# Talking-heads attention with a mixture of experts: w1 of the first expert is loaded two steps apart, and the last tokens' ranks, logits and row numbers get a PSUM bank without transposes

## The chip, the cores and the metric

One core of a Trainium2 chip runs the whole kernel. The metric is the device time of one execution in microseconds (us), less is better. The engines work side by side and wait for one another by semaphores: PE (TensorE, matmuls; its weight loads are PEld), DVE (VectorE), ACT (ScalarE), POOL (GpSimd), and SP (SyncE), which here issues nearly all of the transfers. Matmul results land in PSUM, which is used in banks; all other data lies in SBUF.

## What is computed

The reference, cut to what matters: an attention whose scores are mixed over the 12 heads before and after the softmax, and then, for each of 3584 tokens, one of eight experts, the one with the largest gate logit.

```python
scores = scale * np.matmul(q, k.transpose(0, 1, 3, 2))      # 8 batches, 12 heads, 448 x 448
scores = np.einsum('bhij,hg->bgij', scores, w_pre)
attn = softmax(scores)
attn = np.einsum('bhij,hg->bgij', attn, w_post)
x = np.matmul(attn, v)                                      # as 3584 tokens x 768
logits = x @ w_gate
expert_idx, gate_w = np.argmax(logits, axis=1), largest softmax(logits)
for e in range(8):                                          # w1[e] 768 x 1024, w2[e] 1024 x 768
    xe = x[expert_idx == e]
    out[expert_idx == e] = gate_w * (np.maximum(xe @ w1[e], 0.0) @ w2[e])
```

## The kernel before

The attention runs in 32 query tiles, four for each batch (120, 120, 120 and 88 rows). A tile is worked off in steps of two blocks of query rows (the last of a batch has one block); there are NU = 184 steps. A step turns the scores of its rows into the layout of the mixing (relayout, L288, transfers on SP), mixes over heads (L301), takes the maximum (L307, DVE), the exponential (L315, ACT), scales the post-mixing weights by the sums (L332, POOL), mixes again (`post`, L348), and copies the result out (`evict_p`, L366). When a tile's steps are done, `av` (L408) multiplies by v, `rows` (L428) turns the result into token rows, which go to the DRAM table XD (L442), `choose` finds each token's expert, `rank` (L494) and `place` (L507 to L519) give it a place among the tokens of its expert, and a scatter (L547, POOL) writes its number there.

What runs in which step is a table, filled by `at(step, stage, function)`; within a step the stages run in one fixed order. Stages named in the diff: "fetch" stands near the front, "early" in the middle, "token" and "split_w" late.

The experts compute with float32 numbers split in two, a rounded high part and the rest, and three matmuls for each product. For expert 0 the six parts of w1 (kt 0 to 5, 512 KB each) are prepared while the attention still runs: `fetch_w` loads a part (L581, SP), `round_w` makes its high part ah (L572, ACT), `rest_w` the low part al (L576, on POOL or DVE as the table says). The buffers of the loaded parts are four, so kt 4 waits for the low part of kt 0, and kt 5 for that of kt 1. The table for w1 counts steps back from NU.

After step 184 comes the seam, written out by hand (L835 to L912). In it the last two tiles, T − 1 = 30 and T = 31, finish their token work, and the first 512 tokens of expert 0 are gathered in four slots of 128 rows. Slots 0 and 1 are gathered during the steps. Slots 2 and 3 are gathered by numbers that `patch` (L528) completes with tokens of tile 30; the tokens of tile 31 are added by matmuls with a 0/1 matrix ("hit", L513 and L623). Each slot is turned over on PE (`turn`, L615) into PSUM, in two parts, and then split into high and low parts (`split_x`: cast L630 on ACT, subtraction L631 on DVE, for either part). Then three filler matmuls follow (L189), and the first layer of expert 0 begins (pm_h, L973), for up to 512 tokens at a time; from here on PE works nearly without a gap.

The PSUM names: `bank_m` is the pair that mixing writes, `bank_p` that of the post-mixing, `bank_s` two of two banks each. `side` are the two halves of one bank of bank_s[0]; `bank_r` (ranks), `bank_e` (row numbers of the patch) and, in the change, `bank_g` (gate logits of tile 31) are narrow columns in bank_s[0]. The expert's pools take these banks over when the seam has done with them.

Of the kernel before, what the change touches and what calls it, by code (L numbers as in the profile page):

```python
# [44 lines left out]
def attn_moe_kernel(ctx, tc, qT, kT, v, w_pre, w_post, w_gate, w1, w2, out):  # L45
# [352 lines left out]

    def av(T, groups, first=0):
        b, it, ni = geom[T][:3]  # L400
        chunks = NJ - 1 if ni == IT else NJ
        for n, g in enumerate(groups, first):
            HOME[T, g] = bank_s[1][:, n, :3 * IT].rearrange("p (c i) -> p c i", i=IT)[:, :, :ni]
            for p in range(3):
                for c in range(chunks):
                    for r in range(2):
                        h = 6 * g + 2 * p + r
                        nc.tensor.matmul(out=HOME[T, g][r * D:(r + 1) * D, p, :],  # L408
                                         lhsT=VV[b][:, c, h * D:(h + 1) * D],
                                         rhs=PT[T][:, c, h, :ni], start=(c == 0),  # L410
                                         stop=(c == chunks - 1))
# [36 lines left out]
    bank_r = bank_s[0][:, 1, 496:]  # L448
    bank_g = bank_m[0][:, 480:488]
    bank_e = bank_s[0][:, 1, 488:492]  # L450
# [174 lines left out]

    def split_x(sl, banks):
        for n, (ks, bank) in enumerate(zip(KS, banks)):
            px = bank[:, :(ks.stop - ks.start) * P].rearrange("p (k x) -> p k x", x=P)
# [126 lines left out]
    for kt, (uf, ur, us, engine) in enumerate((  # L755
            (-8, -7, -6, nc.gpsimd), (-7, -6, -5, nc.vector), (-6, -5, -4, nc.gpsimd),
            (-4, -3, None, None), (-3, None, None, None), (-2, None, None, None))):
        at(NU + uf, "fetch", fetch_w, kt)
# [64 lines left out]
    def run(u, *stages):  # L823
        for stage in stages:
            for what in steps.pop((u, stage), []):
                what[0](*what[1:])
# [16 lines left out]
    nc.vector.memset(bank_m[0][JC:, W3], 0.0)  # L843
    run(NU, "evict_r")
    store_x(T - 1)
    choose(T - 1)
    mark(T - 1)
    round_w(4)
    gate(T - 1)
    run(NU, "post")  # L850
    post(*final, banks=bank_m)
    rank(T - 1)
    turn(0, side)
    run(NU, "evict_p")
    evict_p(*final, banks=bank_m)
    place(T - 1)
    round_w(5)
    for g in range(2):
        XT[T, g] = x_p.tile([P, 3, IT], F32, name="xt", bufs=2)
    av(T, (0,))  # L860
    nc.vector.tensor_copy(out=ti2, in_=tb2[:, :, 0].bitcast(I32))
# [3 lines left out]
                                   op1=ALU.mult)  # L865
    split_x(0, side)
    evict_x(T, 0)
    patch(T - 1)
    nc.vector.tensor_tensor(out=tf2, in0=bank_e[:, 0:2], in1=tf2, op=ALU.add)
    nc.vector.tensor_copy(out=ti2, in_=tf2)  # L870
    for n in range(2):
        gather(2 + n, ti2[:, n:n + 1], T - 1)
    token(T - 1)
    number(T - 1)
    scatter(T - 1)
    rest_w(3, nc.vector)
    av(T, (1,), 1)
# [10 lines left out]
    gate(T)  # L888
    turn(1, side)
    place(T)  # L890
    store_x(T)
    nslot = const.tile([P, NE], F32, name="nslot")
# [7 lines left out]
    nc.vector.tensor_copy(out=many, in_=over[:, NE:])  # L900
    split_x(1, side)
    token(T)
    number(T)
    scatter(T)
    turn(2, bank_p, T)
    split_x(2, bank_p)
    turn(3, bank_m, T)
    rest_w(4, nc.vector)
    flags = nc.values_load(many[0:1, 0:1], min_val=0, max_val=(1 << NE) - 1,
                           skip_runtime_bounds_check_because="a sum of different powers of two")  # L910
    split_x(3, bank_m)
    rest_w(5, nc.vector)  # L912
# [238 lines left out]
```

## Time and profile before

| | before |
|---|---|
| time, three runs (us) | 1251.63 median, 1248.43 to 1273.81 |
| the profiled execution (us) | 1252.35 |
| its span, first to last instruction (us) | 1250.6 |
| granted TensorE clock, mean | 0.991 |
| PE busy | 1208.7 us, 97% |
| DVE, ACT, POOL busy | 62%, 55%, 31% |
| steps of the attention end, first expert matmul starts | about 692 and 712.77 us |

Times in the rows below are microseconds from the start of the span. A row of a timeline names start, length, engine, line, operation, "out<-in" and the number of instructions in it; in brackets stands how long the engine was idle just before it, and what released it. "issue" is a time in which the engine waited for nothing that the profile shows. Tile names are the program's: bp, bm and bs are banks of bank_p, bank_m and bank_s, si holds (in the seam) gathered rows and their parts, wraw a loaded part of w1, ah and al its high and low part, et an exponential or a hit matrix.

### The profile page before, as it was taken

How to read it: one execution, taken by the hardware profiler on the slowest of the kernel's cores; microseconds unless marked ns; L12 is line 12 of the kernel's file. 1: busy time of each engine (PE TensorE's matmuls, PEld its weight loads, DVE VectorE, ACT ScalarE, POOL GpSimd, SP SyncE). 2: the span in 40 equal slices, each digit the busy share in tenths (PEclk: the TensorE clock that was granted, in tenths of full speed). 3: DMA queues.
4: the chain of work that ended last, by engine and by line, in shares of the span. 5: the costliest groups of instructions: out<-in, count | busy, mean ns of one | idle time of the engine just before them, and what ended most of it. 6: DMA issues, size and time to landing. Idle time of an engine off the chain costs nothing. (4 is left out here: it accounts for less than half of the span.)

```text
span 1250.6 us, 46569 instructions
## 1 busy us (share of the span) xinstructions
PE 1208.7 (97%) x19601; PEld 1011.5 (81%) x19601; DVE 778.5 (62%) x1977; ACT 683.9 (55%) x1485; POOL 382.8 (31%) x612
## 2 busy tenths in 40 slices
PE   7999999999999999999998899999999999999994
PEld 3677777877777777777776798898989899989894
DVE  5787888878878788788787653434334243535220
ACT  5786878877868687778675342423333242424220
POOL 5443544544535445445334212020201101010000
PEclk9999999999999999999998999999999999999998
DMA  7667657667676676666746364342625344444100
GB/s 201 192 175 183 204 169 204 199 165 211 168 196 193 173 205 198 163 199 175 202 148 185 75 239 160 128 149 86 206 79 172 115 152 142 163 145 157 67 26 34
DMA packets 134858, 200.20 MB, mean 160 GB/s; under 512 B 41637, under 2 KB 112309, under 8 KB 134632
## 3 DMA queue, kind: packets, MB, share of 16 engines
q1 hardware_dynamic: 128438, 172.91, 46.9%
q0 software_dynamic: 6064, 23.86, 5.7%
q8 instruction: 166, 2.72, 0.9%
q14 instruction: 60, 0.49, 0.1%
q10 hardware_dynamic: 130, 0.22, 0.0%
HBM read 97.59 MB, written 23.07 MB: 96 GB/s over the span
## 5 line engine op out<-in xcount | busy, mean ns | idle before, releaser
L315 ACT ACTIVATE et<-bm,st 124x448 f32<-124x448 f32 x360 | 225.4, 631 | 154.8 <-DVE st L307 128.3
L348 PEld LDWEIGHTS bp<-wp,et 60*64 60x64 f32 (+1 forms) x10052 | 198.3, 135 | 76.4 <-issue 56.3
L307 DVE TENSOR_REDUCE st<-bm 124x1 f32<-124x448 f32 x360 | 208.6, 620 | 74.8 <-PE bm L301 66.9
L973 PE MATMUL pm_h<-si,ah 128*128 128x512 f32 (+1 forms) x768 | 228.3, 379 | 1.2 <-PEq L1030 1.0
L366 DVE COPY pt<-bp 128x480 f32<-128x480 f32 x352 | 213.7, 648 | 7.8 <-PE bp L348 6.0
L332 POOL TENSOR_SCALAR wp<-Wpost,st 124x60 f32<-124x60 f32 x360 | 150.9, 434 | 170.6 <-DVE st L325 128.7
L348 PE MATMUL bp<-wp,et 60*64 60x60 f32 (+1 forms) x10052 | 193.0, 219 | 5.1 <-issue 5.1
L301 PE MATMUL bm<-sb,Wquad 60*60 60x448 f32 (+3 forms) x1408 | 186.9, 565 | 4.3 <-ACT et L315 4.3
L278 ACT COPY si<-bs 120x896 f32<-120x896 f32 (+1 forms) x187 | 159.8, 910 | 9.7 <-PE bs L268 9.1
L973 PEld LDWEIGHTS pm_h<-si,ah 128*128 128x128 f32 x768 | 142.6, 188 | 25.7 <-issue 1.7
L1003 POOL DMA_INDIRECT out<-y,ti x30 | 32.5, 1084 | 415.8 <-ACT y L1001 184.2
L973 PE MATMUL pm_h<-si,al 128*128 128x512 f32 (+1 forms) x384 | 144.5, 376 | 0.0
L977 DVE SCALAR_TENSOR_TENSOR hl<-pm_h,hh 128x512 fp32r<-128x512 f32 (+1 forms) x64 | 42.1, 658 | 150.6 <-ACT hh L976 150.1
L408 PE MATMUL bs<-pt,vt 128*64 128x120 f32 (+1 forms) x2496 | 132.2, 260 | 2.6 <-issue 1.4
L976 ACT ACTIVATE hh<-pm_h 128x512 fp32r<-128x512 f32 (+1 forms) x64 | 36.6, 572 | 169.5 <-PE pm_h L973 160.9
L408 PEld LDWEIGHTS bs<-pt,vt 128*64 128x64 f32 x2496 | 118.7, 137 | 7.9 <-issue 2.7
L994 PE MATMUL pm_y<-bh,hh 128*128 128x384 f32 x480 | 124.7, 341 | 0.0
L994 PE MATMUL pm_y<-bh,hl 128*128 128x384 f32 x480 | 122.3, 336 | 0.0
L994 PE MATMUL pm_y<-bl,hh 128*128 128x384 f32 x480 | 122.3, 336 | 0.0
L147 POOL TENSOR_TENSOR ql<-qr,qh 128x360 fp32r<-128x360 f32 (+1 forms) x78 | 69.8, 905 | 166.9 <-ACT qh L146 138.4
L1001 ACT ACTIVATE y<-pm_y,tb 128x384 f32<-128x384 f32 x30 | 17.5, 582 | 145.7 <-PE pm_y L994 87.4
L999 DVE TENSOR_SCALAR y<-pm_y,tb 128x384 f32<-128x384 f32 x30 | 18.5, 615 | 114.9 <-PE pm_y L994 114.9
(175 smaller groups left out, 1786.4 us busy)
## 6 DMA issues: line engine op xcount, KB each, us to landing
sb<-si SPq DMA_DIRECT2D x343, 210.0 KB
wraw<-in_w SPq DMA_DIRECT2D x48, 512.0 KB
wraw<-in_w SPq DMA_DIRECT2D x64, 384.0 KB
vt<-in_v SPq DMA_DIRECT2D x64, 192.0 KB
kr<-in_kT SPq DMA_DIRECT2D x42, 224.0 KB
qr<-in_qT SPq DMA_DIRECT2D x48, 180.0 KB
XD<-xr SPq DMA_DIRECT2D x48, 180.0 KB
sb<-si SPq DMA_DIRECT2D x16, 189.0 KB
```

The costliest lines, as they stand in the source:

```text
L147: engine.tensor_sub(out=lo, in0=src, in1=hi.bitcast(F32))
L278: copy(out=SI[T][:ni, 2 * c:2 * c + 2, :], in_=bank[:ni, :, :S])
L301: nc.tensor.matmul(out=bank_m[r][CUT[c], :S], lhsT=Wquad[CUT[r], CUT[c]], rhs=sb[CUT[r], c, :], start=True, stop=True)
L307: nc.vector.reduce_max(out=st[:R1, 0, c:c + 1], in_=bank_m[c][:R1, :S], axis=AX.X, negate=True)
L315: nc.scalar.activation(out=et[:R1, c, :], in_=bank_m[c][:R1, :S], func=AF.Exp, bias=st[:R1, 0, c:c + 1], scale=1.0, accum_out=st[:R1, 1, c ...
L332: nc.gpsimd.tensor_scalar(out=wp[:R1, c, :], in0=Wpost[:R1], scalar1=st[:R1, 2, c:c + 1], scalar2=None, op0=ALU.mult)
L348: nc.tensor.matmul(out=banks[r][col * JC:(col + 1) * JC, at_:at_ + W], lhsT=et[CUT[r], n, kg * JC:(kg + 1) * JC], rhs=wp[CUT[r], n, :], st ...
L366: nc.vector.tensor_copy(out=flat[:, :, i0 + r * IB:i0 + (r + 1) * IB] .rearrange("p x (n k) -> p x n k", k=IQ), in_=banks[r][:, :2 * NJ * ...
L408: nc.tensor.matmul(out=HOME[T, g][r * D:(r + 1) * D, p, :], lhsT=VV[b][:, c, h * D:(h + 1) * D], rhs=PT[T][:, c, h, :ni], start=(c == 0), ...
L973: nc.tensor.matmul(out=ph[:, :n], lhsT=wx[:, fs], rhs=xx, start=(m == 0), stop=(m == 3 * NK1 - 1))
L977: nc.vector.scalar_tensor_tensor(out=hl[:, ft, :n], in0=ph[:, :n], scalar=0.0, in1=hh[:, ft, :n].bitcast(F32), op0=ALU.max, op1=ALU.subtract)
L994: nc.tensor.matmul(out=py[g][:, :384], lhsT=hx[:, kt, ts], rhs=wx[:, g * 384:(g + 1) * 384], start=(n == 0), stop=(n == 3 * NK2 - 1))
```

## The change

Three things change, all within the last eight steps and the seam.

The table for w1: the loads stand at steps −8, −6, −4, −3, −2 and −1 from the end instead of −8, −7, −6, −4, −3 and −2. Low parts of kt 0 to 2 are all made by POOL; before, kt 1's was made by DVE. The high parts of kt 4 and kt 5 move behind the first split in the seam, and the low parts of kt 3 to 5 are made behind the third and the fourth split.

The banks: the gate logits of tile 31 go to bank_s[0] instead of bank_m[0], and the four turns write bank_p, bank_p, bank_m and `side` instead of `side`, `side`, bank_p and bank_m. So the bank with the ranks, the logits and the row numbers has no transposes until the last turn.

The patch: `av` gets an argument `midway`, a function that it calls after two of its three head pairs. The patch and the two gathers behind it are called there, and the four small operations that prepare their numbers move to the start of the seam.

```diff
-    def av(T, groups, first=0):
+    def av(T, groups, first=0, midway=None):
...
             for p in range(3):
+                if midway and p == 2:
+                    midway()
...
-    bank_g = bank_m[0][:, 480:488]
+    bank_g = bank_s[0][:, 0, 480:488]
...
-    def split_x(sl, banks):
-        for n, (ks, bank) in enumerate(zip(KS, banks)):
+    def split_x(sl, banks, parts=(0, 1)):
+        for n in parts:
+            ks, bank = KS[n], banks[n]
...
     for kt, (uf, ur, us, engine) in enumerate((
-            (-8, -7, -6, nc.gpsimd), (-7, -6, -5, nc.vector), (-6, -5, -4, nc.gpsimd),
-            (-4, -3, None, None), (-3, None, None, None), (-2, None, None, None))):
+            (-8, -7, -6, nc.gpsimd), (-6, -5, -4, nc.gpsimd), (-4, -2, -1, nc.gpsimd),
+            (-3, -1, None, None), (-2, None, None, None), (-1, None, None, None))):
...
     choose(T - 1)
     mark(T - 1)
-    round_w(4)
     gate(T - 1)
...
-    turn(0, side)
     run(NU, "evict_p")
     evict_p(*final, banks=bank_m)
+    turn(0, bank_p)
     place(T - 1)
-    round_w(5)
...
-    av(T, (0,))
...
-    split_x(0, side)
+
+    def numbers():
+        patch(T - 1)
+        split_x(0, bank_p, (0,))
+        nc.vector.tensor_tensor(out=tf2, in0=bank_e[:, 0:2], in1=tf2, op=ALU.add)
+        nc.vector.tensor_copy(out=ti2, in_=tf2)
+        for n in range(2):
+            gather(2 + n, ti2[:, n:n + 1], T - 1)
+
+    av(T, (0,), 0, numbers)
     evict_x(T, 0)
-    patch(T - 1)
-    nc.vector.tensor_tensor(out=tf2, in0=bank_e[:, 0:2], in1=tf2, op=ALU.add)
-    nc.vector.tensor_copy(out=ti2, in_=tf2)
-    for n in range(2):
-        gather(2 + n, ti2[:, n:n + 1], T - 1)
+    split_x(0, bank_p, (1,))
+    round_w(4)
+    round_w(5)
     token(T - 1)
     number(T - 1)
     scatter(T - 1)
-    rest_w(3, nc.vector)
...
-    turn(1, side)
     place(T)
+    turn(1, bank_p)
...
-    split_x(1, side)
+    split_x(1, bank_p)
...
-    turn(2, bank_p, T)
-    split_x(2, bank_p)
-    turn(3, bank_m, T)
-    rest_w(4, nc.vector)
+    turn(2, bank_m, T)
+    split_x(2, bank_m)
+    rest_w(3, nc.vector)
+    turn(3, side, T)
...
-    split_x(3, bank_m)
+    split_x(3, side)
+    rest_w(4, nc.vector)
     rest_w(5, nc.vector)
```

The lines of the kernel after the change stand 2 to 7 higher, so L581 becomes L583, L631 becomes L634 and L973 becomes L980; L348 stays.

On SP, whose transfers start in the order of its queue, the last steps before the change read as follows (wraw<-in_w is a part of w1, sb<-si a relayout, XD<-xr token rows, tb a read of the table of places).

```order
382 L581 DMA wraw<-in_w 128x1024
383 L288 DMA sb_122<-si 120x1x448 x2
384 L442 DMA XD<-xr 120x3x128
385 L581 DMA wraw<-in_w 128x1024
386 L288 DMA sb_119<-si 120x1x448 x2
387 L581 DMA wraw<-in_w 128x1024
388 L288 DMA sb_120<-si 120x1x448 x2
389 L634 DMA tb_133<-TB 128x2x2
390 L288 DMA sb_121<-si 120x1x448
391 L288 DMA sb_121<-si 108x1x448
392 L581 DMA wraw<-in_w 128x1024
393 L288 DMA sb_122<-si 108x1x448
```

After the change the same queue reads:

```order
384 L444 DMA XD<-xr 120x3x128
385 L288 DMA sb_119<-si 120x1x448 x2
386 L583 DMA wraw<-in_w 128x1024
387 L288 DMA sb_120<-si 120x1x448 x2
388 L637 DMA tb_133<-TB 128x2x2
389 L288 DMA sb_121<-si 120x1x448
390 L288 DMA sb_121<-si 108x1x448
391 L583 DMA wraw<-in_w 128x1024
392 L288 DMA sb_122<-si 108x1x448
393 L583 DMA wraw<-in_w 128x1024
394 L444 DMA XD<-xr 120x3x128
395 L583 DMA wraw<-in_w 128x1024
```

One load fewer stands ahead of each of the relayouts sb_119, sb_120 and sb_121, and of the last, sb_122; the last two loads (395 and 397, with one store between) follow the last relayout.

On PE, in the seam, from the ranks of tile 30 to the first ranks of tile 31 (bs_102 is bank_s[0], bs_103 bank_s[1], bp_106 and bp_107 are bank_p, and edge is the patch), before:

```order
4117 L494 MATMUL bs_102<-ohb,ones 128x8
4118 L615 MATMUL bs_102<-ident,si 128x128 x6
4119 L408 MATMUL bs_103<-pt,vt 64x88 x24
4120 L528 MATMUL bs_102<-edge,et 128x1 x2
4121 L408 MATMUL bs_103<-pt,vt 64x88 x24
```

And after:

```order
4117 L496 MATMUL bs_102<-ohb,ones 128x8
4118 L617 MATMUL bp_106<-ident,si 128x128 x2
4119 L617 MATMUL bp_107<-ident,si 128x128 x4
4120 L410 MATMUL bs_103<-pt,vt 64x88 x16
4121 L530 MATMUL bs_102<-edge,et 128x1 x2
4122 L410 MATMUL bs_103<-pt,vt 64x88 x32
```

The first turn goes to another bank, and the patch stands behind 16 of the first 24 rows of av (two matmuls each) instead of behind all of them.

On DVE, at the end of the seam, from the third split to the last low part (bm_104 and bm_105 are bank_m), before:

```order
1647 L631 TENSOR_TENSOR si<-bp_106,si 128x2x128
1648 L631 TENSOR_TENSOR si<-bp_107,si 128x4x128
1649 L576 TENSOR_TENSOR al_13711<-wraw,ah_13710 128x1024
1650 L909 TENSOR_LOAD many
1651 L631 TENSOR_TENSOR si<-bm_104,si 128x2x128
1652 L631 TENSOR_TENSOR si<-bm_105,si 128x4x128
1653 L576 TENSOR_TENSOR al_13817<-wraw,ah_13816 128x1024
```

And after:

```order
1645 L634 TENSOR_TENSOR si<-bm_104,si 128x2x128
1646 L634 TENSOR_TENSOR si<-bm_105,si 128x4x128
1647 L578 TENSOR_TENSOR al_13705<-wraw,ah_13704 128x1024
1648 L915 TENSOR_LOAD many
1649 L634 TENSOR_TENSOR si<-bs_102,si 128x2x128
1650 L634 TENSOR_TENSOR si<-bs_102,si 128x4x128
1651 L578 TENSOR_TENSOR al_13810<-wraw,ah_13809 128x1024
1652 L578 TENSOR_TENSOR al_13912<-wraw,ah_13911 128x1024
```

The last split reads one bank, bs_102, in place of two; kt 3's low part now stands between the third and the fourth split, and kt 4's and kt 5's behind the fourth. The program makes the first expert matmul wait for that fourth split, since its bank passes to the pool of pm_h.

## Rows read from the trace of the kernel before

**Rows 1.** The page: chain that ended last, share of the span by line

```profile
PE pm_y L994 5%; PE pm_h L973 5%; PE pm_x L615 0%; POOL out L1003 0%; DVE y L999 0%; POOLq L1042 0%; POOLq L1030 0%; DVEq L999 0%; POOLq L1003 0%
```

**Rows 2.** Stretches: length, busy us by engine, granted clock, DMA busy, GB/s

```profile
660.00:672.00 12.00, 8.51 (x247) 6.10 (x238) 8.59 (x25) 7.49 (x18) 4.23 (x6) 0.98 0.96 234
```

**Rows 3.** Timeline of PE and one row of ACT, 666 to 680

```profile
666.94 0.87 PE L348 MATMUL bp<-wp,et 64*64 64x60 f32 x46
670.62 0.38 PE L348 MATMUL bp<-wp,et 60*64 60x60 f32 x10 [2.81 <-issue]
...
679.45 0.34 PE L348 MATMUL bp<-wp,et 64*64 64x60 f32 x5 [0.22 <-issue]
...
668.59 0.63 ACT L315 ACTIVATE et<-bm,st 124x448 f32<-124x448 f32 x1
```

**Rows 4.** Stretches: length, PE, PEld, DVE, ACT, POOL, clock, DMA, GB/s

```profile
664.50:671.50 7.00, 4.19 (x106) 2.92 (x102) 3.77 (x9) 4.62 (x11) 2.22 (x3) 1.00 0.94 234
671.50:678.50 7.00, 6.97 (x84) 5.19 (x84) 6.08 (x15) 2.24 (x6) 5.38 (x6) 0.51 0.49 151
678.50:685.50 7.00, 6.26 (x210) 5.21 (x202) 5.67 (x24) 3.16 (x8) 2.93 (x5) 1.00 0.64 189
```

**Rows 5.** Timeline of SP's queue: loads of w1, 661 to 679

```profile
661.31 0.54 SPq L581 DMA_DIRECT2D wraw<-in_w  x1
...
668.55 0.34 SPq L581 DMA_DIRECT2D wraw<-in_w  x1
...
678.04 0.40 SPq L581 DMA_DIRECT2D wraw<-in_w  x1
```

**Rows 6.** Timelines of POOL and of DVE, 675 to 693

```profile
675.13 2.35 POOL L576 TENSOR_TENSOR al<-wraw,ah 128x1024 fp32r<-128x1024 f32 x1
...
692.90 0.43 POOL L332 TENSOR_SCALAR wp<-Wpost,st 124x60 f32<-124x60 f32 x1 [4.12 <-DVE bm L843]
...
676.25 1.26 DVE L323 TENSOR_SCALAR st<-st 124x2 f32<-124x2 f32 x1
...
692.36 0.15 DVE L323 TENSOR_SCALAR st<-st 124x1 f32<-124x1 f32 x1
```

**Rows 7.** Timeline of PE in the seam, 696 to 713

```profile
696.77 2.04 PE L408 MATMUL bs<-pt,vt 128*64 128x88 f32 x48 [1.16 <-DVE pos L507]
700.31 0.61 PE L528 MATMUL bs<-edge,et 120*128 120x1 f32 x4 [1.50 <-DVE si L631]
...
709.83 0.85 PE L615 MATMUL bm<-ident,si 128*128 128x128 f32 x6 [0.42 <-DMA si<-XD,ti]
710.52 1.50 PE L623 MATMUL bm<-et,xr 88*128 88x128 f32 x12
711.86 0.81 PE L189 MATMUL bs<-idle 128*128 128x512 bf16 x3
712.77 0.59 PE L973 MATMUL pm_h<-si,ah 128*128 128x384 f32 x2
```

**Rows 8.** Timelines of ACT and of DVE in the seam, 707 to 712

```profile
707.97 0.37 ACT L630 CAST si<-bs 128x256 fp32r<-128x256 f32 x1 [1.27 <-DVE cbase L519]
709.04 0.59 ACT L630 CAST si<-bs 128x512 fp32r<-128x512 f32 x1 [0.69 <-DVE si L631]
...
708.59 0.41 DVE L631 TENSOR_TENSOR si<-bs,si 128x256 fp32r<-128x256 f32 x1
709.65 0.69 DVE L631 TENSOR_TENSOR si<-bs,si 128x512 fp32r<-128x512 f32 x1 [0.65 <-ACT si L630]
...
711.50 1.21 DVE L576 TENSOR_TENSOR al<-wraw,ah 128x1024 fp32r<-128x1024 f32 x1
```

**Rows 9.** Timeline of PE at 549 and at 17; stretch 20 to 22

```profile
549.02 0.44 PE L348 MATMUL bp<-wp,et 60*64 60x60 f32 x11 [1.41 <-issue]
...
17.30 0.46 PE L268 MATMUL bs<-kh,qh 64*120 64x448 f32 x2 [1.84 <-ACT qh L146]
...
20.00:22.00 2.00, 2.00 (x8) 0.45 (x9) 0.12 (x1) 1.26 (x2) 0.66 (x1) 0.50 1.05 232
```

More of the change, by code (lines that the diff above doesn't have):

```diff
@@ L843, in attn_moe_kernel @@
     nc.vector.memset(bank_m[0][JC:, W3], 0.0)
[L844 to L847, printed above, removed]
-    round_w(4)
[L849 to L852, printed above, removed]
-    turn(0, side)
-    run(NU, "evict_p")
-    evict_p(*final, banks=bank_m)
-    place(T - 1)
-    round_w(5)
-    for g in range(2):
-        XT[T, g] = x_p.tile([P, 3, IT], F32, name="xt", bufs=2)
-    av(T, (0,))
     nc.vector.tensor_copy(out=ti2, in_=tb2[:, :, 0].bitcast(I32))
@@ L865, in attn_moe_kernel @@
                                    op1=ALU.mult)
-    split_x(0, side)
-    evict_x(T, 0)
-    patch(T - 1)
-    nc.vector.tensor_tensor(out=tf2, in0=bank_e[:, 0:2], in1=tf2, op=ALU.add)
-    nc.vector.tensor_copy(out=ti2, in_=tf2)
-    for n in range(2):
-        gather(2 + n, ti2[:, n:n + 1], T - 1)
+    run(NU, "evict_r")
+    store_x(T - 1)
+    choose(T - 1)
+    mark(T - 1)
+    gate(T - 1)
+    run(NU, "post")
+    post(*final, banks=bank_m)
+    rank(T - 1)
+    run(NU, "evict_p")
+    evict_p(*final, banks=bank_m)
+    turn(0, bank_p)
+    place(T - 1)
+    for g in range(2):
+        XT[T, g] = x_p.tile([P, 3, IT], F32, name="xt", bufs=2)
+    def numbers():
[6 more added lines that the diff above has]
+    av(T, (0,), 0, numbers)
+    evict_x(T, 0)
+    split_x(0, bank_p, (1,))
+    round_w(4)
+    round_w(5)
     token(T - 1)
```

## The prediction

> **What bounds the kernel now.** I read the chain of waits first. It follows the end back through the expert matmuls only [rows 1]: from 712.77 us on, TensorE (PE) runs the first layer of expert 0 and goes on almost without a gap to the end [rows 7]. That part, 1250.6 − 712.77 = 537.8 us, is only shifted by this change. So the question is when the matmul of 712.77 can start, and I read backwards from there.
>
> Next come the stretches. From 660 to 672 PE was busy for 8.51 of 12 us while the DMA engines were 0.96 busy and moved 234 GB/s [rows 2], at the place where the change moves loads. PE's own timeline tells more [rows 3]: after 46 of the 56 matmuls of one post-mixing group it stood for 2.81 us, with "issue" as releaser, that is, waiting for nothing the profile shows. The remaining ten use the same operands, so data is no explanation; what can be late is PE's own instructions, which also come over the DMA engines. [...]
>
> The last stretch is the hand-ordered seam, 692 to 713: PE waits 1.16 us for DVE at 696.77 and 1.50 us at 700.31 for a DVE subtraction, and the last turn of gathered rows is done at 710.52 + 1.50 = 712.02 [rows 7].
>
> **The change part by part.**
>
> *Loads two steps apart.* In the new order one w1 load fewer stands ahead of the relayout transfers of the late steps: kt 1 and kt 2 move back a step or two, kt 3 and kt 4 one each, and kt 5 directly behind kt 4 and one 180 KB store. By 234 GB/s [rows 2] a load is 0.524 MB / 234 = 2.2 us of the saturated stretch. If the 2.81 us stand is the backlog of that stretch, 2.2 us less leaves about 0.6 us, and idles of the sort, like the 0.22 at 679.45, left the clock alone [rows 3, 4]. What is that worth? The stand itself: the mixing matmuls behind these ten overwrite a bank that ACT reads in the last exponential, from 668.59 to 669.2 [rows 3], so only 670.6 − 669.2, about 1.5 us, is on the path. The clock: PE's 6.97 us at half speed are 3.5 at full speed, so 3.5 come back if PE alone sets the pace. VectorE (DVE) was busy for 6.08 us of the same 7 [rows 4], and 1.21 of that (kt 1's subtraction, below) moves away: by DVE alone 7 − 4.9 = 2.1 come back. [...] Together −4.5 us, between 0 (the stand stays) and −1.5 − 3.5 = −5, or −6 if the relayouts that land earlier also give steps 182 and 183 some of their waits.
>
> *Subtractions.* kt 1's moves from DVE (1.21 us, as the same operation at 711.50 [rows 8]) to GpSimd (POOL), taking the slot of kt 2's, 2.35 us; kt 2's goes between the last two weighings, where POOL idled 4.12 us before 692.90 [rows 6]. It fits with 1.8 us to spare: 0. A cost could come from sharing: while POOL ran the subtraction at 675.13, a DVE operation that takes 0.15 us elsewhere took 1.26 us [rows 6], 1.1 us lost. That place keeps its cost; in the new slot, about 688.8 to 691.1, DVE reduces and copies out of PSUM, so I take 0, at most 1.1. [...]
>
> *Seam: banks and patch.* With the row numbers in a bank of their own the first turn (0.85 us) no longer stands in it; it is done under the old 1.16 us wait, 0. The patch moves from behind two splits into the middle of the first av group: 696.77 + two thirds of 2.04 = 698.1 instead of 700.31 [rows 7], 2.1 us earlier. Hence the two gathers behind it start 2 us earlier, and the 0.42 us which the last turn waited for one (709.83, "DMA si<-XD" [rows 7]) goes. The second av begins when the first result is copied out, about 700.0 instead of behind the patch at 700.31 + 0.61 = 700.9, and ranks, hits and turns follow 0.9 earlier. The last turn and its hit matmuls then end at 712.02 − 0.9 − 0.42 = 710.7.
>
> *Last subtractions behind the last split.* What the first expert matmul waits for changes. Its PSUM pool takes over the bank in which the last split now lies, so it waits for both halves of that split; before, its last split lay in another bank and DVE finished it after 712.77. I add: cast 0.37, subtraction 0.41, cast 0.59, subtraction 0.69 [rows 8], one after another, because halves of one bank alternated so in the earlier splits (0.65 us waits on each other [rows 8]); and kt 3's subtraction, 1.21 us, ahead of them on DVE until about 711.2, where the first cast has just ended. From there 0.41 + 0.59 + 0.69 with some 0.1 us between each gives about 713.1, and the matmul at about 713.2: +0.45 us. What is queued behind on DVE: kt 4's and kt 5's subtractions (2.4 us, wanted by the 15th and 18th matmul, 14 and 17 matmuls later, at 0.59 / 2 us each [rows 7] over 4 and 5 us: covered) and the slot arithmetic, which ends about 1 us later, under the first expert group. The seam is thus worth +0.3, from −0.8 (the halves overlap) to +1.5. The casts of kt 4 and kt 5 on ACT (1.04 us each) move into its idle time: 0.
>
> *Sum.* 1252.35 − 4.5 + 0.3 = 1248.2. The profiled execution is 0.7 above the median of 1251.63; the prediction for a median is 1247.8.
>
> **Rivals.**
>
> *The stand stays, whatever is loaded.* A stand of 1.41 us with the same releaser, in the middle of the same kind of group, happened at 549.02 with no w1 load near it [rows 9]. Then loads gain nothing and the seam decides: 1252.35 + 0.3 = about 1252. Against it: that one was half as long, at a place with less traffic. [...]
>
> *The stand moves (the slower side).* kt 4 and kt 5 now come back to back with two stores of 180 KB: 1.05 + 0.37 = 1.42 MB or 6 us at 234 GB/s, from about 673 to 679, where before half of it was (kt 5 at 678.04 and two stores, with an idle of 0.22 [rows 3, 5]). If PE stands there for 2.81 us in the open, and the clock falls for 7 us again, the price is 2.8 + 3.5 = 6.3: 1252.35 − 4.5 + 6.3 + 0.3 = 1254.5. It decides once the stand is over 1.5 us: at 1.41 and 1.50 the clock stayed [rows 7, 9], at 2.81 it fell. For it: the traffic; against: the two loads leave no relayout waiting behind them but the very last ones.
>
> *The clock falls at the first expert matmul.* PE would be idle from 710.7 + 0.81 = 711.5, after its three filler matmuls [rows 7], to 713.2: 1.7 us. After an idle of 1.84 us at 17.30, with loose work around it, the clock was 0.50 from 20 to 22 [rows 9]; 1.50 at 700.31 did not [rows 7]. PE is the bound there, so 3.5 to 7 us at half clock (7 as in [rows 4], or half of it) cost 1.75 to 3.5 us in full: 1248 + 2.6 = 1250.5.
>
> *More than I count.* The halves of the last split overlap, and the seam's earlier patch shows in full (−0.8), with −6 in the steps: 1252.35 − 6.8 = 1245.5.
>
> **How the numbers follow.** Chances: forecast 0.45, the stand stays 0.16, the stand moves 0.13, the clock at the expert matmul 0.13, more than I count 0.11, anything else 0.02. The likeliest case's own range is 1246.3 to 1250; with the cases of both signs the range goes from 1244 to 1254, which leaves out the upper end of the moved stand and the far ends. All the change can touch lies between 650 and 720 us, and the most any case moves is 7 us or 0.6%. A measurement of this kernel can tell about 2% from no change, 25 us; no case reaches that, so 0.97 is for within 2%, 0.015 for either side.
>
> **What would show it.** Right: no "issue" idle over 1.5 us on L348 between 660 and 690, a granted clock of 1.00 there, and the last post-mixing group 4 to 5 us earlier in the span. In the seam: patch matmuls inside the av group, no DMA wait at the last turn, and the first expert matmul waiting for a DVE subtraction, 0.4 us later counted from the last post-mixing group. Wrong: a stand and a clock of 0.50 between 673 and 682; or a granted clock under 1.00 in the 10 us after the first expert matmul; or a stand of 2 us or more at the old place with one load fewer ahead of it, which would take the load out of the explanation.

## The result and the profile after

The changed kernel is slower: 1260.56 us in the median of 20 runs, against 1251.78 of 20 before; the ratio is 1.0058, with a 95% interval from 1.0037 to 1.0079. The ratio is that of the means without the executions in a slower state of the chip (one before, three after), so it is below that of the medians. I had predicted 1247.8, so the sign is wrong and the time lies outside the range (1244 to 1254). The profiled execution took 1258.23 us with a span of 1256.5 (1252.35 and 1250.6 before).

Not all of those 5.9 us of span are the change's. In the part of the program that both kernels share, the first eight post-mixing matmuls of one late step (L348 x8, behind the first six mixing matmuls) start at 662.27 before and at 664.47 after: 2.2 us were gone before anything differs. I take these eight matmuls as the zero point from here on. They and the end of the last post-mixing (L348 x28) on PE, before and after:

```profile
662.27 0.39 PE L348 MATMUL bp<-wp,et 64*64 64x60 f32 x8
693.38 0.69 PE L348 MATMUL bm<-wp,et 64*64 64x60 f32 x28
```

```profile
664.47 0.39 PE L348 MATMUL bp<-wp,et 64*64 64x60 f32 x8
692.85 0.64 PE L348 MATMUL bm<-wp,et 64*64 64x60 f32 x28
```

The stretches of the profiled execution after, with the columns of [rows 4]:

```profile
660.00:672.00 12.00, 9.97 (x284) 7.46 (x280) 9.53 (x35) 6.28 (x18) 5.09 (x8) 1.00 0.82 229
672.00:692.00 20.00, 16.10 (x398) 12.63 (x391) 14.85 (x49) 9.35 (x23) 12.37 (x14) 1.00 0.58 160
692.00:713.00 21.00, 18.36 (x252) 16.80 (x252) 10.86 (x55) 7.09 (x16) 3.89 (x5) 0.76 0.27 70
713.00:735.00 22.00, 20.27 (x111) 19.67 (x111) 13.89 (x32) 6.78 (x12) 5.59 (x5) 0.92 0.66 205
```

The first two rows are the steps: PE is busy for 9.97 instead of 8.51 us of the first [rows 2] (a window that lies 2.2 us earlier in this program than in the one before), and the clock of 0.51 [rows 4] is gone. The last two are the seam and the first expert matmuls, and now the clock is low there. PE's timeline shows both. First the steps:

```profile
669.14 0.87 PE L348 MATMUL bp<-wp,et 64*64 64x60 f32 x46
671.39 0.38 PE L348 MATMUL bp<-wp,et 60*64 60x60 f32 x10 [1.38 <-issue]
...
678.42 0.52 PE L348 MATMUL bp<-wp,et 64*64 64x60 f32 x21 [1.39 <-issue]
...
684.36 0.51 PE L348 MATMUL bp<-wp,et 64*64 64x60 f32 x20 [1.34 <-issue]
...
690.03 0.45 PE L348 MATMUL bp<-wp,et 64*64 64x60 f32 x13 [0.97 <-issue]
```

The stand of 2.81 us [rows 3] has become 1.38, at the very same place behind 46 matmuls, but three more follow. Then the seam, and the stretches in it where the clock is low:

```profile
698.79 1.01 PE L530 MATMUL bs<-edge,et 120*128 120x1 f32 x4
699.73 1.44 PE L410 MATMUL bs<-pt,vt 128*64 128x88 f32 x16
701.71 3.79 PE L410 MATMUL bs<-pt,vt 128*64 128x88 f32 x48 [0.54 <-DVE xt L421]
...
712.72 1.50 PE L625 MATMUL bs<-et,xr 88*128 88x128 f32 x12
714.06 0.81 PE L189 MATMUL bs<-idle 128*128 128x512 bf16 x3
716.60 0.98 PE L980 MATMUL pm_h<-si,ah 128*128 128x384 f32 x2 [1.73 <-DVE si L634]
```

```profile
696.10:706.40 10.30, 9.62 (x107) 8.98 (x108) 3.29 (x15) 2.45 (x3) 3.15 (x3) 0.50 0.29 77
706.40:716.60 10.20, 7.83 (x66) 6.90 (x66) 6.83 (x27) 3.91 (x10) 1.01 (x1) 1.00 0.12 31
716.60:720.00 3.40, 3.40 (x11) 3.40 (x12) 3.18 (x9) 0.00 (x0) 0.00 (x0) 0.50 0.50 97
```

The patch stands inside av, as wanted, and the last turn waits for no DMA any more. But the 48 av matmuls behind it take 3.79 us instead of 2.04, because the granted clock is 0.50 from 696.1 to 706.4; and the first expert matmul waits 1.73 us for a subtraction of the last split and then starts at half clock. Against the zero point the changed kernel is 2.8 us ahead at the end of the last post-mixing (693.49 − 664.47 = 29.0 us, before 694.07 − 662.27 = 31.8). It needs 23.1 us from there to the first expert matmul, where the kernel before needs 18.7: 4.4 us lost.

These two distances, "steps" and "seam", cut the program at the border of the change's two halves and leave out what happens earlier, so I use them for all traces (us; a trace is one execution):

| kernel | table | seam's code | steps | seam | clock at 0.50 between 660 and 722 | ratio to before, interval |
|---|---|---|---|---|---|---|
| before | old | old | 31.8 | 18.7 | 671.6–678.4 | |
| g1, before again | old | old | 30.2 | 19.0 | 671.5–674.9, 695.4–698.8 | 1.0032 (0.9991–1.0074) |
| e1 | new | old | 28.7 | 18.8 | 694.0–697.4 | 0.9994 (0.9950–1.0037) |
| after | new | new | 29.0 | 23.1 | 696.1–706.4, 716.6–720.0 | 1.0058 (1.0037–1.0079) |
| g2, after again | new | new | 28.7 | 22.7 | 671.3–674.7, 702.0–708.8 | 1.0057 (1.0014–1.0099) |
| e4, shifted | new | new | 27.9 | 22.8 | 706.9–713.7 | |
| e2 | old | new | 29.6 | 21.4 | 704.6–708.0, 714.8–718.2 | 1.0039 (1.0000–1.0077) |
| e3, fillers | new | new | 28.6 | 20.6 | none | 1.0027 (0.9985–1.0069) |
| f1, subtraction moved | new | mended | 28.8 | 18.9 | none | |
| f2, banks | new | mended | 25.9 | 18.0 | none | |
| f3, scatter later | new | mended | 26.4 | 18.8 | 707.0–710.5 | |
| f4, three mends | new | mended | 26.4 | 19.2 | none | 1.0013 (0.9970–1.0056) |
| g3, banks and scatter | new | mended | 28.5 | 17.8 | none | 0.9996 (0.9953–1.0038) |
| h1, as g3 | old | mended | 32.2 | 17.9 | 672.0–675.4, 685.6–689.1 | 1.0021 (0.9976–1.0065) |

### The profile page after: what moved, and what is told of

Same layout as the page of the kernel before. It is cut to its first block, busy times and chain, and to the rows that moved or that the text cites. A ratio compares the mean times of both kernels' runs of the same rounds, so it can differ in the third digit from the quotient of the medians.

```text
span 1256.5 us, 46568 instructions
## 1 busy us (share of the span) xinstructions
PE 1211.0 (96%) x19601; PEld 1014.7 (81%) x19601; DVE 776.8 (62%) x1976; ACT 683.7 (54%) x1485; POOL 385.4 (31%) x613
## 5 line engine op out<-in xcount | busy, mean ns | idle before, releaser
L348 PEld LDWEIGHTS bp<-wp,et 60*64 60x64 f32 (+1 forms) x10052 | 197.7, 135 | 79.1 <-issue 57.2
L980 PE MATMUL pm_h<-si,ah 128*128 128x512 f32 (+1 forms) x768 | 229.8, 381 | 2.8 <-DVE si L634 1.7
L348 PE MATMUL bp<-wp,et 60*64 60x60 f32 (+1 forms) x10052 | 193.0, 219 | 7.7 <-issue 7.5
L980 PEld LDWEIGHTS pm_h<-si,ah 128*128 128x128 f32 x768 | 143.7, 189 | 26.7 <-ACT si L633 2.2
L980 PE MATMUL pm_h<-si,al 128*128 128x512 f32 (+1 forms) x384 | 144.8, 377 | 0.0
L410 PE MATMUL bs<-pt,vt 128*64 128x120 f32 (+1 forms) x2496 | 134.8, 265 | 2.3 <-issue 1.6
L410 PEld LDWEIGHTS bs<-pt,vt 128*64 128x64 f32 x2496 | 122.0, 140 | 6.8 <-issue 2.2
```

The costliest lines, as they stand in the source:

```text
L348: nc.tensor.matmul(out=banks[r][col * JC:(col + 1) * JC, at_:at_ + W], lhsT=et[CUT[r], n, kg * JC:(kg + 1) * JC], rhs=wp[CUT[r], n, :], st ...
L410: nc.tensor.matmul(out=HOME[T, g][r * D:(r + 1) * D, p, :], lhsT=VV[b][:, c, h * D:(h + 1) * D], rhs=PT[T][:, c, h, :ni], start=(c == 0), ...
L980: nc.tensor.matmul(out=ph[:, :n], lhsT=wx[:, fs], rhs=xx, start=(m == 0), stop=(m == 3 * NK1 - 1))
```

## The experiments

**e1 and e2: each half alone.** e1 is the kernel before with the new table, e2 the changed kernel with the old one. The edit of e1 (e2 is the reverse, in the changed kernel):

```diff
-            (-8, -7, -6, nc.gpsimd), (-7, -6, -5, nc.vector), (-6, -5, -4, nc.gpsimd),
-            (-4, -3, None, None), (-3, None, None, None), (-2, None, None, None))):
+            (-8, -7, -6, nc.gpsimd), (-6, -5, -4, nc.gpsimd), (-4, -2, -1, nc.gpsimd),
+            (-3, -1, None, None), (-2, None, None, None), (-1, None, None, None))):
```

> The kernel before with the changed table for w1 alone (loads, high parts, low parts); the seam as it was. In the trace of the changed kernel the steps from the last mixing of step 180 to the ranks of tile 30 went 2.7 to 4 us faster than before, measured against the point just ahead (offset +2.20 us at 668.34, -1.37 at the mixing of 675.59, -0.53 at the ranks), and all the loss came behind that. Theory A (the seam costs, the table gains): ratio 0.996 to 0.999, the first expert matmul about 3 us earlier than in the kernel before, clock 1.00 from 660 to 692, stands of 1.0 to 1.4 us on PE at the same four places. Rival B (the four stands of PE that the table brings lower the clock afterwards, so the table is what costs): ratio 1.003 or more, a granted clock of 0.50 somewhere between 690 and 720 though the seam is the old one.

> The changed kernel with the old table for w1, so the change of banks, patch and order in the seam alone. Theory A: ratio 1.005 to 1.009, the old stand of about 2.8 us near 670 with the clock at 0.50 behind it, the first expert matmul waiting 1.5 to 2 us for the last subtraction on DVE, and the clock at 0.50 at least once between 692 and 722. Rival B: ratio 0.998 to 1.002, since the seam by itself moves the first expert matmul by less than 1 us.

e1 came out at 0.9994 and e2 at 1.0039, whose interval begins at 1.0000; both lie between the ranges of the two theories, and with these widths the ratios alone separate nothing. The distances do: e1's steps take 28.7 us with the clock at 1.00 from 660 to 692, its seam 18.8; e2's seam takes 21.4. That is theory A, but for two details. e2, with the old table, stood 1.66 and 1.43 us, not 2.8, so the size of the stand varies from run to run. And e1's clock did fall, from 694.0 on, in the old seam: that is the sign which rival B had named, but it cost that seam nothing that can be seen (18.8 against 18.7). e2 also showed a wait that the slow clock had hidden in the changed kernel. The rows of its PE, DVE and POOL, with the copies of both av results (L421):

```profile
699.11 2.04 PE L410 MATMUL bs<-pt,vt 128*64 128x88 f32 x48 [0.54 <-DVE xt L421]
...
703.51 0.93 PE L430 MATMUL bs<-xg,xt 128*88 128x136 f32 x6 [1.79 <-DVE xt L421]
...
698.63 0.43 DVE L421 COPY xt<-bs 128x264 f32<-128x264 f32 x1 [0.40 <-PE bs L410]
703.02 0.43 DVE L421 COPY xt<-bs 128x264 f32<-128x264 f32 x1 [3.06 <-remote]
...
698.50 1.09 POOL L650 DMA_INDIRECT si<-XD,ti  x1 [5.78 <-DVE ti L871]
...
701.22 1.04 POOL L549 DMA_INDIRECT TB<-tg,di  x1 [0.31 <-issue]
```

av is done at 701.15, and the copy of its result (L421), which by the program waits for nothing else, starts 1.9 us later, 0.76 us behind the end of POOL's scatter (702.26). f3 takes that up.

**e3: fillers.** The changed kernel with more filler matmuls where PE waits in the seam:

```diff
     post(*final, banks=bank_m)
+    keep_clock(bank_s[1][:, 1, :], 3)
     rank(T - 1)
+    keep_clock(bank_s[1][:, 1, :], 2)
...
     av(T, (0,), 0, numbers)
+    keep_clock(bank_s[1][:, 1, :], 2)
...
-    keep_clock(bank_s[1][:, 0, :], 3)
+    keep_clock(bank_s[1][:, 0, :], 10)
```

> The changed kernel with more filler matmuls on an unused PSUM bank where PE waits in the seam: three ahead of the ranks of tile 30, two behind them, two between the av groups, and ten instead of three ahead of the first expert matmul. If the loss is the granted clock (10.2 us at half speed from 696.1 in the seam and 3.4 us from 716.6 on, which cost some 4 and 1.7 us), the clock stays at 1.00 from 690 to 735 and the time falls by 4 to 6 us against the changed kernel: ratio to before 0.999 to 1.002. If the loss lies in the waits themselves, the fillers change nothing: ratio 1.005 to 1.007.

The clock stayed at 1.00 from 692 to 713, and the seam took 20.6 us instead of 23.1; 1.9 us of the loss against before stayed. That the fillers held the clock is not shown: in eight other traces with the new seam (e2, e4, g2, f1 to f3, g3, h1) it stayed up without them through the same short waits at the seam's start. Nor are the 2.5 us the clock's whole share, since e3 waits 1.29 us for the second copy, which the trace of the changed kernel did not: against f1 below, which has neither that wait nor the slow clock, the changed kernel lost 4.2 us. The stretch of e3 from 692 to 713:

```profile
692.00:713.00 21.00, 18.04 (x273) 14.99 (x276) 13.29 (x60) 7.84 (x18) 4.89 (x6) 1.00 0.25 70
```

And its PE timeline, with the copy on DVE:

```profile
704.24 0.93 PE L430 MATMUL bs<-xg,xt 128*88 128x136 f32 x6 [1.29 <-DVE xt L421]
...
703.75 0.43 DVE L421 COPY xt<-bs 128x264 f32<-128x264 f32 x1 [2.56 <-PE bs L410]
...
712.20 2.10 PE L189 MATMUL bs<-idle 128*128 128x512 bf16 x9
714.52 0.58 PE L983 MATMUL pm_h<-si,ah 128*128 128x384 f32 x2 [0.22 <-DVE si L634]
```

Fillers take the place of the wait at the end; the expert matmul starts no earlier, 2.38 us behind the last hit matmuls (710.64 + 1.50) as without them. So both explanations are right in part: there are waits of 1.3 to 1.7 us, and there is a clock that falls. The ratio, 1.0027, lies between the two ranges and cannot say more.

**e4: what the stands are.** 32 tiny matmuls ahead of everything:

```diff
     keep_clock(bank_p[0], 12)
+    for _ in range(32):
+        nc.tensor.matmul(out=bank_p[0][:, :8], lhsT=idle[:, :P], rhs=idle[:, :8], start=True, stop=True)
```

> The changed kernel with 32 tiny matmuls (64 instructions with their weight loads) ahead of the first work of PE, where it waits for loads anyway. In the trace the four stands of PE between 668 and 691 lie at the records 32706, 32962, 33218 and 33474 of PE, exactly 256 apart. If they are waits for blocks of 256 instructions, they come 64 instructions earlier in the program: behind 14 instead of 46 matmuls of the post-mixing near 670, and the others 32 matmuls earlier too. If a stand belongs to its place (its operands, its banks), it stays behind 46.

The PE timeline of e4 at the first stand:

```profile
672.92 0.40 PE L348 MATMUL bp<-wp,et 64*64 64x60 f32 x14
674.68 0.85 PE L348 MATMUL bp<-wp,et 60*64 60x60 f32 x42 [1.36 <-issue]
```

It stands behind 14, as the block theory has it; the later three were under 0.4 us here and could not be compared. So a stand is PE waiting for its next 256 instructions. The stand of 1.41 us at 549.02, which I had held against this reading [rows 9], lies on the same grid: its record is 24 times 256 ahead of the one at 670.62 (26562 and 32706).

The trace holds the transfers of the instructions too. The page of the kernel before has them in a queue of their own (packets, MB, share of the 16 DMA engines):

```profile
q8 instruction: 166, 2.72, 0.9%
```

That is 16 KB a packet. One packet ran from 668.04 to 669.26, and PE went on at 670.62, 1.36 us behind its end; in the changed kernel one ran from 668.84 to 669.88, and PE went on at 671.39, 1.51 us behind. At every stand on the grid between 660 and 692, in all fourteen traces, PE goes on 1.25 to 1.69 us behind the end of such a packet; at 549.02 it was 1.67 us (the packet ended at 547.35). Where PE came to such a place later than that, it did not stand: in the kernel before at 678.89 and 684.35, 2.07 and 1.89 us behind the ends of their packets (676.82 and 682.46). So the stands of up to 2.81 us show where PE came to a block before it was there.

**f1: one subtraction moved.** kt 3's subtraction at its old place:

```diff
     scatter(T - 1)
+    rest_w(3, nc.vector)
     av(T, (1,), 1)
...
     split_x(2, bank_m)
-    rest_w(3, nc.vector)
```

> The changed kernel with kt 3's subtraction back at its old place, behind the first av group. In four traces of the new seam the first expert matmul follows the last hit matmul by 2.38 us (after: 714.22 to 716.60) with 1.73 us of waiting for the second half of the last split on DVE; before, it was 0.75 us. If kt 3's subtraction (1.21 us) between the third and the fourth split is what makes DVE late, the distance falls by about 1.1, to 1.2 to 1.4 us, and the wait to about 0.6. If the four alternating operations of the split in one bank (0.37, 0.41, 0.59, 0.69 us) are enough by themselves, it stays above 2 us.

The subtraction made no difference: the expert matmul still waits 1.71 us, 2.36 us behind the last hit matmuls. The four alternating operations of the split are enough by themselves; DVE had the time for kt 3. The seam is 18.9 us here for another reason: the second copy followed av at once (702.77, with the scatter at 702.79), and the clock held. The last hit matmuls end 16.5 us behind the last post-mixing, where the prediction had 710.7 − 694.07 = 16.6. The timelines of f1's DVE, POOL and PE:

```profile
702.77 0.43 DVE L421 COPY xt<-bs 128x264 f32<-128x264 f32 x1
711.60 0.42 DVE L634 TENSOR_TENSOR si<-bs,si 128x256 fp32r<-128x256 f32 x1 [1.01 <-ACT si L633]
712.67 0.69 DVE L634 TENSOR_TENSOR si<-bs,si 128x512 fp32r<-128x512 f32 x1 [0.65 <-ACT si L633]
...
702.79 1.04 POOL L549 DMA_INDIRECT TB<-tg,di  x1 [0.31 <-DVE al L578]
...
713.51 0.59 PE L980 MATMUL pm_h<-si,ah 128*128 128x384 f32 x2 [1.71 <-DVE si L634]
```

**f2: the bank of the last split.**

```diff
-    turn(2, bank_m, T)
-    split_x(2, bank_m)
+    turn(2, side, T)
+    split_x(2, side)
...
-    turn(3, side, T)
+    turn(3, bank_m, T)
...
-    split_x(3, side)
+    split_x(3, bank_m)
```

> The changed kernel with the third turn in the halves of the ranks' bank and the fourth in bank_m, as the fourth was before. If the first expert matmul waits only because its pool takes over the bank in which the last split lies, the wait of 1.73 us for DVE at that matmul is gone (0 to 0.3 us; 0.75 us from the last hit matmul, as before), and the third turn waits up to 0.8 us for the reads of the ranks. If the splits themselves are the limit whatever the bank, the wait stays at 1.5 us or more.

The timelines of f2's PE, DVE and POOL:

```profile
702.23 0.85 PE L617 MATMUL bs<-ident,si 128*128 128x128 f32 x6 [1.25 <-ACT si L633]
...
704.91 1.50 PE L625 MATMUL bm<-et,xr 88*128 88x128 f32 x12
706.47 0.59 PE L189 MATMUL bs<-idle 128*128 128x512 bf16 x2
707.17 0.58 PE L980 MATMUL pm_h<-si,ah 128*128 128x384 f32 x2
...
697.26 0.43 DVE L421 COPY xt<-bs 128x264 f32<-128x264 f32 x1 [1.24 <-PE bs L410]
...
697.29 1.04 POOL L549 DMA_INDIRECT TB<-tg,di  x1 [0.31 <-issue]
```

The wait at the expert matmul is gone, 0.76 us from the last hit matmuls as before. So the bank made it wait; the turn now pays 1.25 us in its place, more than the 0.8 I had allowed.

**f3: the copy and the scatter.** The gate values that the scatter of tile 30 waits for move behind the second copy:

```diff
-    token(T - 1)
-    number(T - 1)
-    scatter(T - 1)
     av(T, (1,), 1)
     evict_x(T, 1)
+    token(T - 1)
+    number(T - 1)
+    scatter(T - 1)
     logits(T, 0)
```

> The changed kernel with the gate values of tile 30, which its scatter waits for, behind the second copy out of av on DVE. In three traces of the new seam at full clock that copy (L421, bank bs) starts 0.74 to 0.78 us behind the end of the scatter on POOL, 1.3 to 1.8 us behind the av matmuls it needs, and PE waits 1.29 to 1.79 us for it at the first token rows (703.51 in e2). If the transfers that POOL prepares hold the copy up, the wait falls to 0.6 us or less. If the copy waits for something else, it stays at 1.3 us or more. Where the granted clock is 0.50 there, as in the trace of the changed kernel, the wait doesn't show; then the copy's start against the end of the scatter decides.

The copy now starts 0.05 us behind av (695.77), and PE has no wait there. The timelines of f3's DVE and POOL:

```profile
695.77 0.43 DVE L421 COPY xt<-bs 128x264 f32<-128x264 f32 x1 [1.54 <-PE bs L410]
...
696.83 1.04 POOL L549 DMA_INDIRECT TB<-tg,di  x1 [1.34 <-DVE tg L544]
```

So the wait goes with the scatter's place: with the scatter behind the copy it is gone, here and in f4, g3 and h1. How the scatter would delay the copy is not shown. It is not a copy that already has its signal: in e3 the profile names PE's av as what ended the copy's wait (703.75), and in e2, e4 and g2 the semaphore of PE on which the copy waits is counted up 0.02 us ahead of the copy, 1.70 to 1.84 us behind the modelled end of the last av matmul (1.35 in e3). In f1 and f2 it is counted up 0.02 us behind that end. So the signal that av is done came late, or av itself, whose end the profile only models. The visible times do not say when this happens: av ends 0.07 to 0.08 us ahead of the scatter's start in e2, e4 and g2, where the copy waited, and just so in f1 and f2, where it did not; and the first copy of e2 started 0.13 us behind the start of a gather on POOL (698.63 and 698.50) with a wait of 0.40 us, for PE's av.

**f4: three mends.** f1, f3 and the fillers together (five at the end).

```diff
     round_w(5)
+    rest_w(3, nc.vector)
+    av(T, (1,), 1)
+    evict_x(T, 1)
     token(T - 1)
     number(T - 1)
     scatter(T - 1)
-    av(T, (1,), 1)
-    evict_x(T, 1)
...
     split_x(2, bank_m)
-    rest_w(3, nc.vector)
```

> The changed kernel with three mends together: kt 3's subtraction at its old place, the scatter of tile 30 behind the second copy, and the fillers (three ahead of the ranks, two behind them, two between the av groups, five at the end). If the losses of the new seam are the 1.73 us and the 1.3 to 1.8 us of waiting and the clock that falls behind them, the distance from the last post-mixing to the first expert matmul is 17 to 18.5 us (18.7 before, 23.1 in the trace of the changed kernel, 20.6 with fillers alone), and the ratio to before 0.995 to 1.000. If something else in the change costs, 1.003 or more stays.

The seam took 19.2 us, 0.7 more than expected at most: the split's bank still keeps the expert matmul 2.36 us behind the hit matmuls, and the fillers ahead of the second av delay it by about 0.4. The clock held. The ratio, 1.0013, lies between the two readings and settles neither.

**g1 and g2: both kernels again, unchanged.**

> The kernel before, unchanged: a second trace of it, and the spread of a ratio where nothing differs (0.997 to 1.003 expected). Reading A: the 2.81 us stand of PE near 670 and the 6.8 us at half clock behind it belong to the one profiled execution (with the same old table, e2 stood 1.66 and 1.43 us and kept the clock). Then here the stretch from matmul 16000 (662.27) to the end of the last post-mixing is about 29 us, not 31.8, the clock stays at 1.00 from 660 to 690, and the table had little to gain. Reading B: they belong to the kernel; then a stand of 2.5 us or more and a clock of 0.50 show again.

> The changed kernel, unchanged: a second trace. The first expert matmul follows the last hit matmul by 2.3 to 2.4 us whatever the clock (that is in the program); the distance from the last post-mixing to it is 18.9 us where the second copy out of av wins its race against the scatter and the clock holds, 20.5 to 21.4 where the copy loses, up to 23.1 where the clock falls too. Ratio 1.003 to 1.008.

g1 stood 2.67 us at the old place with the clock at half speed behind it, though for 3.4 us only. So the stand belongs to the kernel (reading B), and the length of the low clock to the run. Just as telling is its ratio: the kernel before against itself gave 1.0032, from 0.9991 to 1.0074. In the same comparison the changed kernel gave 1.0057; the medians of 12 runs each were 1258.87 and 1263.35. The stand in g1's PE timeline:

```profile
670.20 0.38 PE L348 MATMUL bp<-wp,et 60*64 60x60 f32 x10 [2.67 <-issue]
```

In g2 the second copy came late and then the clock fell, as its POOL, DVE and PE show, and behind them the stretch from 702:

```profile
699.48 1.04 POOL L549 DMA_INDIRECT TB<-tg,di  x1 [0.31 <-issue]
...
701.13 0.43 DVE L421 COPY xt<-bs 128x264 f32<-128x264 f32 x1 [2.91 <-remote]
...
701.62 1.34 PE L430 MATMUL bs<-xg,xt 128*88 128x136 f32 x6 [1.64 <-DVE xt L421]
```

```profile
702.00:708.80 6.80, 6.80 (x36) 6.77 (x35) 3.27 (x19) 2.10 (x6) 0.00 (x0) 0.50 0.17 44
```

**g3 and h1: a seam without the two losses, with either table.** The turns use bank_p, bank_m, bank_p, bank_m, so that none lies in the ranks' bank, and the scatter stands as in f3 (h1: the old table). The splits read the banks of their turns.

```diff
-    turn(1, bank_p)
+    turn(1, bank_m)
...
-    turn(2, bank_m, T)
+    turn(2, bank_p, T)
...
-    turn(3, side, T)
+    turn(3, bank_m, T)
```

> The changed kernel with the turns in bank_p, bank_m, bank_p, bank_m (none in the ranks' bank), and the gate values of tile 30 behind the second copy. If the bank of the last split and the race of copy and scatter are the two losses of the new seam, the first expert matmul follows the last hit matmul by 0.7 to 1.0 us, and the last post-mixing by 17 to 18 us (18.7 before, 18.8 with the scatter alone moved); ratio 0.995 to 0.999. If the ranks' bank was not what made the first expert matmul wait, 2.3 us stay.

> The mended seam of g3 (alternating banks, scatter behind the second copy) with the old table for w1: the table alone, the other way round. From matmul 16000 of PE to the end of the last post-mixing the three traces with the old table took 31.80, 30.16 and 29.56 us, the nine with the new one 25.9 to 29.0 (mean 27.9). If the table gains what the traces say, it takes 29.5 us or more here, with a stand of 1.6 to 2.8 us near 670; if the seam was behind that, under 29. From there to the first expert matmul it takes 17.5 to 18 us if the seam's mends carry by themselves (17.75 in g3, 18.70 to 18.97 in the seam before). Ratio 0.998 to 1.003 by rows, which five rounds can hardly tell from 1: the same kernel before against itself gave 1.0032 with an interval from 0.9991 to 1.0074.

The end of g3's seam on PE, and the stand in h1's PE timeline:

```profile
702.25 1.50 PE L625 MATMUL bm<-et,xr 88*128 88x128 f32 x12
703.59 0.81 PE L189 MATMUL bs<-idle 128*128 128x512 bf16 x3
704.55 0.58 PE L980 MATMUL pm_h<-si,ah 128*128 128x384 f32 x2
```

```profile
670.03 0.38 PE L348 MATMUL bp<-wp,et 60*64 60x60 f32 x10 [2.81 <-issue]
```

g3's expert matmul starts 0.80 us behind the last hit matmuls, and the seam takes 17.8 us, about 1 us less than the old one; h1 repeats it with 17.9. h1's steps take 32.2 us with the stand of 2.81 us back. By rows g3 has the shortest seam of these kernels, and steps like the others with the new table. By its time (0.9996, from 0.9953 to 1.0038, and a median 1.6 us under that of g1 in the same comparison) it is no faster than before as far as these runs can tell, and one comparison of the kernel with itself was off by as much as its gain should be.

## Why the prediction was wrong

**The bound.** Right, as far as these traces can tell: from the first expert matmul on, the kernel before took 537.8 and 538.7 us (g1), the changed one 539.9 and 537.9 (g2), and of the 539.9 some 1.7 are the half clock in the first 3.4 us. What counted was when that matmul starts.

**Loads two steps apart: −4.5, measured about −3.** Right in sign and cause. With the old table the steps took 31.8, 30.2, 29.6 and 32.2 us, mean 30.9; with the new one ten traces gave 25.9 to 29.0, mean 27.9, and no trace of either is among the other's. The step that was off is "2.2 us less leaves about 0.6": 1.1 to 1.4 us stayed in all ten. The packet of instructions for this place starts 5.7 to 5.8 us behind the zero point in the kernel before, g1 and h1 (4.6 in e2), and 3.9 to 4.4 us behind it in the ten, so a load fewer brought it forward by some 1.5 us, not 2.2. The prediction had no row for the refill; the trace of the kernel before had it, in the packet that ended at 669.26. A PE that neither stands so long nor runs at half clock also comes to the next blocks sooner, and stands there: 1.39, 1.34 and 0.97 us in the changed kernel, while the kernel before, at half clock until 678.4, came to these three places 2.07, 1.89 and 4.71 us behind the ends of their packets (at 678.89, 684.35 and 690.60) and stood at none; in g2, whose clock was low from 671.3, they are gone too. The rival "the stand moves" had this in it, but put it down to kt 4 and kt 5 and as one stand with a clock drop; in the trace of the changed kernel it was three small ones, and no drop. "The stand stays, whatever is loaded" is refuted: the loads about halve it. Of the stand, 670.6 − 669.2 = 1.4 us were on the path, where the sum had 1.5. No run shows the 3 us that the sum took for the half clock: with the old table the steps took 29.6 us in e2, where the clock held in them behind a stand of 1.66 us, and 30.2, 31.8 and 32.2 us with 3.4, 6.8 and 6.9 us of half clock behind stands of 2.67 to 2.81 us (g1, before, h1).

**Subtractions: 0.** Nothing in the traces speaks against it: no DVE wait appears near kt 2's new place.

**Seam: +0.3 predicted, +3.7 measured.** The old seam took 18.7, 19.0 and 18.8 us; the new one, with no mend, 23.1, 22.7 and 22.8 and, with the old table, 21.4, mean 22.5. This is the term that failed. By its steps:

- The earlier patch was right: at full clock the gate logits of tile 31 start 7.9 us behind the last post-mixing, before 8.75 to 8.9 us: 0.8 to 1.0 gained.
- "Ranks, hits and turns follow 0.9 earlier" failed. The scatter that comes earlier with the patch now starts just when av ends, and in e2, e3, e4 and g2 the second copy comes late there and PE waits 1.3 to 1.8 us for it; in the trace of the changed kernel itself the clock was low there instead. I had weighed what the subtraction moved to POOL could disturb, not what the transfers brought forward could. Where neither happened, in the one trace of f1, the sum held: 18.9 us, against 18.7 + 0.3 predicted.
- The last split's distance was right, as a sum and in its cause: 713.2 − 710.7 = 2.5 us predicted from the last hit matmuls, 2.38 measured. The one bank makes the matmul wait (f2, g3); kt 3's subtraction has no part in it (f1), as the sum had it. But these 1.6 us more were to be paid by 1.3 us gained ahead of them, and that gain did not come. (The working gave +0.45 us for the seam, and the sum took +0.3.)
- The clock was a rival with 0.13, tied to the idle ahead of the expert matmul. Of the four unmended traces two fell there (after and e2, at 716.6 and 714.8), and all four fell earlier in the seam. In three of these (g2, e2, e4) that was within 1.1 us behind the copy's wait of 1.6 to 1.8 us. In the trace of after it fell at 696.1, behind waits of 0.69, 0.44 and 0.21 us, and eight other traces kept it behind the same waits. Why it fell there stays open.

**The sum and its base.** I reckoned against one execution. Its gains were real, but the same rows in other executions vary by more than what I was adding up: the stand between 1.66 and 2.81, the half clock behind it between nothing and 6.8 us.

**What stays open.** By rows the change is worth −3.0 + 3.7 = +0.7 us up to the first expert matmul, and about 1.7 more where that starts at half clock. From the zero point to the end the traces took 588.3 and 587.9 us before, 592.0 and 589.3 after. The times say 0.58%, some 7 us, from 0.37 to 0.79%. The unchanged kernel's 1.0032 shows that part of it may be the comparison; that is one comparison, whose interval holds 1. Whether the remaining microseconds lie in the seam's worse executions or elsewhere, these traces, one or two for each kernel, do not show. The zero point itself lies anywhere from 658.3 to 668.2 us in the fourteen traces, and in the comparisons of twelve the profiled execution was always among the four fastest (g2: 1253.73 us, the median 1263.35). So what lengthens most executions is in no trace here.

## What to carry to other kernels

Where a stand on PE has no releaser, count the instructions between stands: here an even spacing of 256, with a packet of the instruction queue landing 1.25 to 1.69 us ahead of each restart, was PE waiting for its program. A load fewer ahead of it shortened the stand from between 1.66 and 2.81 us to between 1.1 and 1.4, though PE then met the next ones (1.39, 1.34 and 0.97 us in the changed kernel). When work is brought forward, list what else runs and which banks are in use at the new time; here a scatter that moved to the end of av went with waits of up to 1.8 us in four traces, and a bank handed from the last split to the first expert matmul cost 1.6. Gains of a few microseconds in 1250 are judged by distances between two instructions that both kernels share, in several traces, and with the kernel compared against itself.

## What the runs showed of the hardware that I had not expected

PE waits for its own instructions in blocks of 256, for up to 2.81 us (the DMA engines were 0.94 busy around that stand [rows 4]), and goes on 1.25 to 1.69 us behind the packet that brings them. In e2, e3, e4 and g2 PE's signal that av is done was counted up 1.35 to 1.84 us late, 0.6 to 0.8 us behind the recorded end of the scatter that POOL prepares, though the program does not connect the two; the cause is open. And the granted clock fell behind single waits of PE of 1.64 to 1.79 us (702.0 in g2, 704.6 in e2, 706.9 in e4, 707.0 in f3), yet not behind 1.71 us in f1 or the 1.50 us of the kernel before [rows 7]. It fell behind 1.15 and 1.16 us in the old seam as well (694.0 in e1, 695.4 in g1), where the kernel before kept it behind the same 1.16 [rows 7]: the length of one wait alone does not decide it.
